# The low halves of the experts' weights formed on GpSimd instead of VectorE, except for the first expert's first matrix

## The chip, the cores and the metric

The kernel runs on one core of a Trainium2 chip. The metric is the device time of one execution in microseconds (us), the median of several runs. The names of the engines are those of the profile: PE is TensorE (PEld its weight loads), DVE is VectorE, ACT is ScalarE, POOL is GpSimd, SP is SyncE. L820 is line 820 of the kernel.

## The reference

The input of 8 sequences of 2496 tokens with 256 channels is filtered in the frequency domain, and the 19968 tokens that result are each sent to one of 8 experts, at most 2496 to each, in the order of their logits. An expert is two matrix products with a ReLU between them.

```python
X = np.fft.rfft(x, axis=1)
y = np.fft.irfft(X * (filt_r + 1j * filt_i)[None], n=2496, axis=1)
x = y.reshape(19968, 256)
logits = x @ w_gate                       # 8 experts
# greedy assignment: largest logits first, at most 2496 tokens for each expert
for e in range(8):
    mask = assigned == e
    out[mask] = np.maximum(x[mask] @ w1[e], 0.0) @ w2[e]
```

## The kernel before

The first part, up to about 400 us, transforms, filters and transforms back, and computes the logits. The second part is the experts, one after the other, and this is where the change lies. In it PE's instructions stand in the order in which the code issues them; the orders on DVE, ACT and POOL come from a scheduler that goes by its own estimates of time.

All products are made in a format with fewer mantissa bits, and to keep the accuracy each operand is split in two: a high half (the operand rounded to the format) and a low half (the operand minus its high half). A product is then three matmuls: high by high, high by low, low by high.

The weights of expert `e` are fetched with two indirect DMAs issued on POOL (L810, tiles `wr`): 128 partitions by 2048 elements for each of the two matrices. `Ffn.split` then makes the halves in eight parts of 512 columns, four for the first matrix and four for the second. For a part ACT writes the high half (L819, tiles `w0h` and `w1h`), and the low half is the difference (L820, `w0l` and `w1l`). The halves have two buffers each, so those of the next expert are made while PE still works on this one. The list `split` is worked off one part at a time between PE's steps, the first matrix's four parts first.

An expert's 2496 tokens are taken in five groups, four of 512 and one of 448. POOL gathers a group's rows with four indirect DMAs (L826, `xg`), PE transposes them (L840, `ptr`), and ACT and DVE split the result (L843 `xo`, L844 `z`). `first` makes eight products with the first matrix (L862, `pz`); for each, ACT writes the high half of the ReLU (L868) and DVE the low half (L870, or L873 in two pieces for the last group; tile `hl`). Then come the products with the second matrix (L905, `py`), the copy to `y` on ACT (L915) and the scatter to the output with an indirect DMA on POOL (L916).

While expert `e` runs, the assignment for the next one is made on DVE, with small matmuls on PE in between (`Route.phase` and `places`): rounds of counting with `Gm` (L553) and `rt` (L561, L574), then a table of tokens in five chunks (L757 to L789) that ends in the indices `xid`, for which the gathers wait. Some long DVE instructions over the logits belong to it: L638, L640, L642, L645 and L649. All of this falls mostly at the change from one expert to the next, when the new weights are split too.

So POOL's queue in the second part holds the weight loads (L810), the gathers (L826) and the scatters (L916), and DVE's queue holds the low halves of weights, of inputs and of ReLUs together with the assignment. Each engine works its own queue strictly in order.

Of the kernel before, what the change touches and what calls it, by code (L numbers as in the profile page):

```python
# [7 lines left out]
F32, F32R = mybir.dt.float32, mybir.dt.float32r  # L8
BF, F16, I32 = mybir.dt.bfloat16, mybir.dt.float16, mybir.dt.int32
AF, OP, AX = mybir.ActivationFunctionType, mybir.AluOpType, mybir.AxisListType  # L10
# [123 lines left out]
class Fft:  # L134
# [132 lines left out]
    def split(s, b, q, v, eng):  # L267
        y = s.yd[b, q] = [s.wp.tile([128, 2, D], F32R, name=n, bufs=3) for n in ("yh", "yl")]
        s.nc.scalar.copy(y[0], v)
        eng.tensor_tensor(y[1], v, y[0].bitcast(F32), op=OP.subtract)  # L270
# [522 lines left out]
class Ffn:  # L793
# [18 lines left out]
    def split(s, e, part):  # L812

        nc = s.nc
        raw, hl = s.wt[e]
        k, h = divmod(part, 4)
        o = 512 * (h if k else 2 * (h % 2) + h // 2)
        src, hi, lo = (t[:, o:o+512] for t in (raw[k], *hl[k]))
        nc.scalar.copy(hi, src)  # L819
        nc.vector.tensor_tensor(lo, src, hi.bitcast(F32), op=OP.subtract)  # L820

    def gather(s, e, g, ids):
        for t in range(4*g, 4*g + 4):
# [103 lines left out]
def emit(tc, i, out):  # L927
    nc = tc.nc
    with ExitStack() as st:
# [91 lines left out]
        while len(split) > 6:  # L1021
            W.split(*split.pop(0))
# [8 lines left out]
        with tc.manual_schedule(engines={mybir.EngineType.PE}):  # L1031
            pump.until((0, 1))
            p = ps.tile([128, 2, 256], F32, name="ptr", tag="c", bufs=4)
            for _ in range(12):
                nc.tensor.matmul(p[:, 0, :128], hot, hot, start=True, stop=True)
            for h in range(2):
                R.last = W.turn(0, 0, h)
            with tc.issue_after(R.last):
                while len(split) > 2:
                    W.split(*split.pop(0))  # L1040
            for e in range(8):
                pump.limit = e + 1
                def hook(what):
                    if what == 'w2':
                        flush(8)
                    elif isinstance(what, tuple):
                        gather(e, what[1])
                    elif e < 7:
                        if what == 'last':
                            gather(e + 1, 0)  # L1050
                            flush(4)
                        else:
                            W.turn(e + 1, 0, what - 1)
                for pe in W.run(e, pump, hook):
                    pump.feed(pe)
                    n += 1

                    if split and n % PACE == 0:
                        with tc.issue_after(W.lasta):
                            W.split(*split.pop(0))  # L1060
# [85 lines left out]
```

## Time and profile before

| what | value |
|---|---|
| median of 3 runs | 1422.28 us (1421.41 to 1422.91) |
| the profiled execution | 1421.22 us, of which the span is 1419.4 us |
| TensorE clock granted, mean of the span | 0.991 of full speed |
| PE busy | 1381.1 us, 97% of the span |
| DVE busy | 892.7 us, 63% |
| ACT busy | 675.1 us, 48% |
| POOL busy | 482.4 us, 34% |

The table is to be read with care: busy shares are averages over the span, and the parts of it differ. PE is near full throughout; what can still change the end is the little time in which it waits.

### The profile page before, as it was taken

The numbers are of one execution on the slowest core, as the hardware profiler recorded it, in microseconds if no ns is written. First come the engines' busy times: TensorE is split into PE (matmuls) and PEld (weight loads), VectorE is DVE, ScalarE is ACT, GpSimd is POOL, SyncE is SP. The second block draws the span as 40 slices with busy tenths as digits, with TensorE's granted clock in tenths as the row PEclk, the third lists the DMA queues.
The fourth block names the chain that finished last, engine by engine and source line by source line (L and its number), as shares of the span: only waits on it lengthen the run. The fifth ranks groups of instructions, "written<-read, shape, count | busy, mean of one in ns | idle before, by whom it ended". The sixth has DMA issues, their size and how long they took to land.

```text
span 1419.4 us, 27197 instructions
## 1 busy us (share of the span) xinstructions
PE 1381.1 (97%) x10362; PEld 1212.0 (85%) x10362; DVE 892.7 (63%) x2548; ACT 675.1 (48%) x1638; POOL 482.4 (34%) x539
## 2 busy tenths in 40 slices
PE   9999999999969999999999999999999999999998
PEld 8998898975438897898888989898898999899988
DVE  5577676775556768758757876876867635423231
ACT  6766666645455236326425534633723635423231
POOL 3343343431024125323531632433333323323312
PEclk9999999999989999999999999999999999999999
DMA  9665664537882022102212212112111321111100
GB/s 376 242 232 180 203 212 136 162 141 248 300 297 70 21 82 69 41 27 94 62 40 75 73 44 82 53 47 91 54 38 49 127 67 52 47 42 51 39 20 29
DMA packets 56532, 153.11 MB, mean 108 GB/s; under 512 B 9409, under 2 KB 29905, under 8 KB 52817
## 3 DMA queue, kind: packets, MB, share of 16 engines
q1 hardware_dynamic: 28072, 69.46, 14.0%
q0 software_dynamic: 18416, 60.37, 12.9%
q10 hardware_dynamic: 9913, 21.53, 4.3%
q8 instruction: 82, 1.34, 0.4%
q14 instruction: 49, 0.40, 0.1%
HBM read 88.32 MB, written 63.06 MB: 107 GB/s over the span
## 4 chain that ended last, share of the span: by engine, by line
PE 84%; issue 6%; DVE 4%; DMA 3%; ACT 2%; POOL 1%; POOLq 0%; ACTq 0%; DVEq 0%
PE py L905 27%; PE pz L862 27%; PE p L213 5%; PE p L229 5%; PE pv L393 4%; PE pa L284 4%; PE pa L248 2%; PE rt L561 2%; PE ptr L840 2%; PE pv L257 2%; POOL out L916 1%; DMA z<-zd 1%; PE rt L772 1%; DVE hl L873 1%; DMA wr<-w,widx 1%
## 5 line engine op out<-in xcount | busy, mean ns | idle before, releaser
L905 PE MATMUL py<-w1h,hl 128*128 128x256 f32 x2496 | 483.7, 286 | 1.1 <-DVE hl L873 1.0
L905 PEld LDWEIGHTS py<-w1h,hl 128*128 128x128 f32 x2496 | 401.3, 191 | 4.3 <-DVE hl L873 1.9
L905 PE MATMUL py<-w1l,hl 128*128 128x256 f32 (+1 forms) x1280 | 358.9, 282 | 0.0
L916 POOL DMA_INDIRECT out<-y,oid x160 | 167.0, 1044 | 490.1 <-ACT y L915 431.1
L868 ACT ACTIVATE hl<-pz 128x512 fp32r<-128x512 f32 (+1 forms) x320 | 188.1, 588 | 233.1 <-PE pz L862 208.2
L862 PE MATMUL pz<-xo,w0h 128*128 128x512 f32 (+1 forms) x640 | 263.3, 411 | 3.3 <-DVE dr L736 1.6
L870 DVE SCALAR_TENSOR_TENSOR hl<-pz,hl 128x512 fp32r<-128x512 f32 x256 | 175.1, 687 | 130.5 <-ACT hl L868 129.2
L862 PE MATMUL pz<-z,w0h 128*128 128x512 f32 (+1 forms) x640 | 248.6, 388 | 0.6 <-DVE z L844 0.6
L862 PE MATMUL pz<-xo,w0l 128*128 128x512 f32 (+1 forms) x640 | 248.4, 388 | 0.0
L905 PEld LDWEIGHTS py<-w1l,hl 128*128 128x128 f32 (+1 forms) x1280 | 240.9, 188 | 2.0
L826 POOL DMA_INDIRECT xg<-xs,xid x160 | 166.6, 1041 | 134.1 <-issue 55.7
L915 ACT COPY y<-py 128x256 f32<-128x256 f32 x152 | 56.6, 372 | 298.6 <-PE py L905 252.4
L862 PEld LDWEIGHTS pz<-xo,w0l 128*128 128x128 f32 x640 | 120.6, 188 | 23.8
L862 PEld LDWEIGHTS pz<-xo,w0h 128*128 128x128 f32 x640 | 121.5, 190 | 20.9 <-issue 2.1
L862 PEld LDWEIGHTS pz<-z,w0h 128*128 128x128 f32 x640 | 121.5, 190 | 16.8 <-DVE z L844 1.6
L219 ACT COPY Y<-p 64x240 f32<-64x240 f32 (+1 forms) x302 | 115.3, 382 | 29.3 <-PE p L213 22.2
L237 POOL TENSOR_TENSOR P<-P 128x256 f32<-128x256 f32 x80 | 58.7, 734 | 163.1 <-DVE P L235 162.9
L553 DVE TENSOR_TENSOR Gm<-M,thr 117x1232 bf16<-117x1232 f32 (+2 forms) x80 | 105.5, 1329 | 0.2
L213 PE MATMUL p<-cS,xr 117*128 117x120 f32 x688 | 93.9, 276 | 2.7 <-ACT Y L219 1.5
L213 PEld LDWEIGHTS p<-cS,xr 117*128 117x128 f32 x688 | 85.4, 191 | 6.8 <-ACT Y L219 4.3
L229 PE MATMUL p<-cW,Y 128*128 128x128 f32 x640 | 88.4, 276 | 0.6 <-DVE Q L236 0.6
L229 PEld LDWEIGHTS p<-cW,Y 128*128 128x128 f32 x640 | 80.0, 191 | 5.7 <-issue 3.9
(221 smaller groups left out, 1992.5 us busy)
## 6 DMA issues: line engine op xcount, KB each, us to landing
z<-zd SPq DMA_DIRECT2D x26, 600.0 KB
zd<-zt SPq DMA_DIRECT2D x60, 256.0 KB
xs<-xo ACTq DMA_DIRECT2D x18, 600.0 KB
xr<-x SPq DMA_DIRECT2D x6, 1536.0 KB
xr<-x SPq DMA_DIRECT2D x6, 1216.0 KB
zd<-zt ACTq DMA_DIRECT2D x20, 256.0 KB
xs<-xo SPq DMA_DIRECT2D x8, 600.0 KB
xr<-x SPq DMA_DIRECT2D x8, 512.0 KB
```

What stands on the lines that cost most here:

```text
L213: s.lastmm = nc.tensor.matmul(p[:, q-q0, :120], xv[:, q-24*h], s.cS1, start=True, stop=True).ins
L219: c = (nc.vector.tensor_copy if (t == 5 if b else cp) else nc.scalar.copy)(dst, src)
L229: nc.tensor.matmul(p[:, k], s.Y1[b][:, 4*g+k, dh*128:dh*128+128], s.cW[:, 4*g+k], start=True, stop=True)
L237: nc.gpsimd.tensor_tensor(P[:, :, :64], P[:, :, :64], P[:, :, 64:], op=OP.subtract)
L284: s.nc.tensor.matmul(p, w, v, start=m == 0, stop=m == 2)
L553: nc.vector.tensor_tensor(Gm[:, s0:s1, :m], s.M[:, s0:s1].unsqueeze(2).to_broadcast([117, s1 - s0, m]), thr[:117].unsqueeze(1).to_broadcas ...
L826: s.lastg = s.nc.gpsimd.indirect_dma_start(out=xg[:n], out_offset=None, in_=s.xs, in_offset=bass.IndirectOffsetOnAxis(ap=ids[0][:n, t:t+1] ...
L862: nc.tensor.matmul(p[:, :n], w[:, sl], x[:, k, :n], start=m == 0, stop=m == 5)
L868: s.lasta = s.R.relu = nc.scalar.activation(h[:, :n], p[:, :n], AF.Relu).ins
L870: s.R.low = nc.vector.scalar_tensor_tensor(l[:, :n], p[:, :n], 0.0, h[:, :n].bitcast(F32), op0=OP.max, op1=OP.subtract).ins
L905: nc.tensor.matmul(p[:a.stop-a.start], hs[g][f][:, a], b[:, 256*f:256*f+256], start=m == 0, stop=m == 8 * len(terms) - 1, skip_group_check ...
L916: st = nc.gpsimd.indirect_dma_start(out=out_rows, out_offset=bass.IndirectOffsetOnAxis(ap=ids[1][:w, 4*g+t:4*g+t+1], axis=0), in_=y[:w], i ...
```

## The change

The low half of a weight part is formed on POOL instead of DVE, for the second matrix of every expert and for the first matrix of all experts but the first. That is 60 instructions of 64; four, of the first expert's first matrix, stay on DVE. The operation, its operands and the high halves on ACT are as before.

```diff
         src, hi, lo = (t[:, o:o+512] for t in (raw[k], *hl[k]))
         nc.scalar.copy(hi, src)
-        nc.vector.tensor_tensor(lo, src, hi.bitcast(F32), op=OP.subtract)
+        (nc.gpsimd if e or k else nc.vector).tensor_tensor(lo, src, hi.bitcast(F32), op=OP.subtract)
```

The scheduler sets the orders anew. PE's and SP's are the same as before; those of POOL, DVE and, a little, ACT are not. On POOL, from the weight loads for the second expert on (`wr_6577` and `wr_6578` are its two raw matrices), the rows before were:

```order
L810 DMA wr_6577<-w,widx 128x2048
L810 DMA wr_6578<-w,widx 128x2048
L916 DMA out<-y,oid 19968x256 x4
L826 DMA xg<-xs,xid 128x256 x4
L916 DMA out<-y,oid 19968x256
L826 DMA xg<-xs,xid 128x256 x4
L916 DMA out<-y,oid 19968x256 x2
```

After the change the same place reads as follows, from behind the two weight loads on.

```order
L916 DMA out<-y,oid 19968x256 x2
L820 TENSOR_TENSOR w0l<-wr_6577,w0h 128x512 x2
L916 DMA out<-y,oid 19968x256
L820 TENSOR_TENSOR w0l<-wr_6577,w0h 128x512
L916 DMA out<-y,oid 19968x256
L826 DMA xg<-xs,xid 128x256 x4
L820 TENSOR_TENSOR w0l<-wr_6577,w0h 128x512
L820 TENSOR_TENSOR w1l<-wr_6578,w1h 128x512 x2
L916 DMA out<-y,oid 19968x256
L820 TENSOR_TENSOR w1l<-wr_6578,w1h 128x512
L916 DMA out<-y,oid 19968x256
L826 DMA xg<-xs,xid 128x256 x4
```

Eight low halves have come into POOL's queue, three ahead of the first gathers of the new expert and four more ahead of the second; the eighth stands behind those. On DVE, at the same change of experts and behind the low halves of the last group's ReLUs (`hl`), the rows before were:

```order
L737 TENSOR_TENSOR r<-r_6451,dr 128x8
L820 TENSOR_TENSOR w1l<-wr_6578,w1h 128x512
L773 TENSOR_TENSOR loc<-sidx,rt 128x2
L873 SCALAR_TENSOR_TENSOR hl<-pz,hl 128x64
L873 SCALAR_TENSOR_TENSOR hl<-pz,hl 128x384
L873 SCALAR_TENSOR_TENSOR hl<-pz,hl 128x64
L873 SCALAR_TENSOR_TENSOR hl<-pz,hl 128x384
L773 TENSOR_TENSOR loc<-sidx,rt 128x2
L765 TENSOR_SCALAR GE<-iota,BC 117x512
L873 SCALAR_TENSOR_TENSOR hl<-pz,hl 128x64
L873 SCALAR_TENSOR_TENSOR hl<-pz,hl 128x384
L727 TENSOR_TENSOR asg<-asg,u_6713 117x176
```

And with the change, from the same L737 on:

```order
L737 TENSOR_TENSOR r<-r_6451,dr 128x8
L773 TENSOR_TENSOR loc<-sidx,rt 128x2
L873 SCALAR_TENSOR_TENSOR hl<-pz,hl 128x64
L873 SCALAR_TENSOR_TENSOR hl<-pz,hl 128x384
L873 SCALAR_TENSOR_TENSOR hl<-pz,hl 128x64
L873 SCALAR_TENSOR_TENSOR hl<-pz,hl 128x384
L773 TENSOR_TENSOR loc<-sidx,rt 128x2
L765 TENSOR_SCALAR GE<-iota,BC 117x512
L727 TENSOR_TENSOR asg<-asg,u_6713 117x176
L733 TENSOR_TENSOR val<-val,a_6718 128x8
L873 SCALAR_TENSOR_TENSOR hl<-pz,hl 128x64
L873 SCALAR_TENSOR_TENSOR hl<-pz,hl 128x384
```

The low half of the weights is gone from between L737 and L773, and the last pair of ReLU halves now stands behind L727 and L733.

## Rows read from the trace of the kernel before

**Rows 1.** The page: busy time and share of the span, by engine.

```profile
PE 1381.1 (97%) x10362; PEld 1212.0 (85%) x10362; DVE 892.7 (63%) x2548; ACT 675.1 (48%) x1638; POOL 482.4 (34%) x539
```

**Rows 2.** Windows: stretch, its length, busy time of each engine, clock, DMA.

```profile
539.20:557.20 18.00, 15.66 (x115) 14.20 (x115) 17.75 (x59) 9.47 (x31) 10.34 (x9) 1.00 0.22 67
...
1200.00:1300.00 100.00, 100.00 (x679) 92.23 (x678) 31.78 (x89) 35.69 (x88) 32.33 (x34) 1.00 0.13 42
```

**Rows 3.** PE's timeline behind 440 us: every wait, in brackets with its releaser.

```profile
540.05 0.44 PE L862 MATMUL pz<-xo,w0h 128*128 128x448 f32 x1 [1.59 <-DVE dr L736]
...
545.71 0.50 PE L905 MATMUL py<-w1h,hl 128*128 128x256 f32 x2 [0.70 <-DVE hl L873]
...
547.24 0.50 PE L905 MATMUL py<-w1h,hl 128*128 128x256 f32 x2 [0.30 <-DVE hl L873]
...
557.31 0.50 PE L862 MATMUL pz<-z,w0h 128*128 128x512 f32 x1 [0.59 <-DVE z L844]
...
569.67 0.64 PE L561 MATMUL rt<-A,Gm 117*128 117x96 bf16 x11 [0.89 <-DVE Gm L553]
...
671.87 0.33 PE L772 MATMUL rt<-dt,GE 117*128 117x180 f16 x2 [1.49 <-DVE ex L777]
...
896.78 0.51 PE L862 MATMUL pz<-xo,w0h 128*128 128x512 f32 x1 [0.98 <-DVE loc L773]
...
919.75 0.42 PE L561 MATMUL rt<-A,Gm 117*128 117x48 bf16 x10 [0.38 <-DVE ex L777]
...
1025.87 0.45 PE L561 MATMUL rt<-A,Gm 117*48 117x32 bf16 x11 [0.94 <-DVE ex L777]
```

**Rows 4.** Line 820: count, ns (min/median/max), starts; DVE's idle time before it.

```profile
L820 DVE TENSOR_TENSOR w0l<-wr,w0h x32: 675/684/721, 419.3 to 1196.4; 128x512 fp32r<-128x512 f32 x32
...
  ACT w0h L819: 15.9, 11
```

**Rows 5.** Groups on POOL by form: count, busy us, mean ns, idle before.

```profile
L270 POOL TENSOR_TENSOR yl<-Y,yh 128x512 fp32r<-128x512 f32 x4 | 5.0, 1277 | 16.9 <-PE pa L284 14.9 <-ACT yh L269 2.0
```

**Rows 6.** DVE's timeline: start and length in us.

```profile
329.84 1.02 DVE L589 TENSOR_TENSOR thr<-km,ic 128x7 int32<-128x7 int32 x1
330.90 2.58 DVE L553 TENSOR_TENSOR Gm<-M,thr 117x560 bf16<-117x560 f32 x2
...
454.51 0.17 DVE L589 TENSOR_TENSOR thr<-km,ic 128x7 int32<-128x7 int32 x1
...
544.32 0.67 DVE L820 TENSOR_TENSOR w1l<-wr,w1h 128x512 fp32r<-128x512 f32 x1
544.92 0.14 DVE L773 TENSOR_TENSOR loc<-sidx,rt 128x2 f32<-128x2 f32 x1
```

**Rows 7.** POOL's timeline at the same place as the first two rows of group 6.

```profile
329.55 1.29 POOL L270 TENSOR_TENSOR yl<-Y,yh 128x512 fp32r<-128x512 f32 x1 [1.95 <-ACT yh L269]
331.50 1.26 POOL L270 TENSOR_TENSOR yl<-P,yh 128x512 fp32r<-128x512 f32 x1 [0.66 <-PE pa L284]
```

**Rows 8.** Groups on DVE from 539.2 to 557.2 us: busy us, mean ns.

```profile
L873 DVE SCALAR_TENSOR_TENSOR hl<-pz,hl 128x64 fp32r<-128x64 f32 (+1 forms) x12 | 4.0, 372 | 0.0
L820 DVE TENSOR_TENSOR w1l<-wr,w1h 128x512 fp32r<-128x512 f32 x4 | 2.7, 674 | 0.0
L640 DVE TENSOR_TENSOR tmp<-lg,M 117x1408 f32<-117x1408 f32 x1 | 1.6, 1606 | 0.0
```

**Rows 9.** POOL's timeline: gathers for the second expert.

```profile
541.71 2.45 POOL L826 DMA_INDIRECT xg<-xs,xid  x1 [0.30 <-PE pz L862]
...
550.99 0.97 POOL L826 DMA_INDIRECT xg<-xs,xid  x1 [1.68 <-PE ptr L840]
```

**Rows 10.** Timelines of ACT and PE at three places.

```profile
433.16 0.61 ACT L819 CAST w1h<-wr 128x512 fp32r<-128x512 f32 x1
...
440.30 0.28 PE L905 MATMUL py<-w1l,hl 128*128 128x256 f32 x1
...
562.54 0.60 PE L840 MATMUL ptr<-id,xg 128*128 128x128 f32 x4
```

## The prediction, made before the changed kernel ran

> **What bounds the kernel now.** I read the page first for the busy shares [rows 1]: PE is busy 97% of the span, no other engine more than 63%. So PE's own work sets the time, and since the change leaves PE's instructions and their order as they are, it can reach the end only through the time in which PE waits. The reader should therefore look next not at DVE's 893 us but at PE's timeline in the part that the change touches, from about 440 us on, and pick out the rows with a bracket [rows 3]. There are nine. They add up to 1.59 + 0.70 + 0.30 + 0.59 + 0.89 + 1.49 + 0.98 + 0.38 + 0.94 = 7.86 us, and in every one the releaser is DVE. They come in bunches: five between 540 and 570 (first to second expert), one at 672, two around 900 to 920, one at 1026, each at a change of experts. The windows view says why [rows 2]: from 539.2 to 557.2 DVE is busy 17.75 us of 18, while between 1200 and 1300, when no weights are split for a next expert and the counting is over, it is busy 31.8 of 100 and PE waits for nothing. So DVE is the limit for some 18 us at a time, at the changes of experts, and nowhere else behind 440 us. Of those 18 us five low halves of weights are a part: the four of the second matrix, 2.7 us of busy time [rows 8], and the last one of the first matrix.
>
> All that is to be gained is hence at most 7.9 us of 1422, 0.55%. A measurement of this kernel tells about 0.2%, 2.84 us, from no change.
>
> **What is removed.** Sixty low halves leave DVE. The instruction is 0.68 us long in the median [rows 4], but the next one starts a little before it ends: 0.60 us after it at 544.32 [rows 6]. So one takes 0.60 us of DVE's queue, and 60 of them are 36 us, nearly all of it work beside which PE runs on. DVE also sat idle for 15.9 us in front of eleven of the `w0l` [rows 4], which tells that the first ones of an expert come at a time when DVE has nothing else to do: taking those away gives PE nothing. What counts is the last five of an expert, which stand in the full stretch: 5 x 0.60 = 3.0 us. The first expert's four that move (the second matrix) have no wait of PE near them: no row of [rows 3] lies before 540.
>
> **What is added on POOL.** The same operation in the same shape, 128x512 with two float operands in SBUF, stands in the trace on POOL already, in L270: 1.277 us [rows 5]. Sixty are 77 us, on an engine busy 34% of the span [rows 1]. That is cover enough on average; the question is what stands behind them in the queue. These are scatters, for which nobody waits soon, and gathers. The second four gathers of the second expert begin at 550.99 us [rows 9], and PE transposes the first of them at 562.54 [rows 10]: from the end of the first issue 10.6 us, for a transfer and for whatever comes in between. The order puts four low halves between the first and the second four gathers, 4 x 1.28 = 5.1 us. They fit, even if POOL were idle for none of it; cost nothing, with some 5 us to spare. For the first expert, ACT's last cast of the second matrix starts at 433.16 and takes 0.61; one POOL instruction later it is 435.1, and PE first reads a low half of that matrix at 440.30 [rows 10]: nothing. The low halves of the later experts are made before the expert begins or during its first group, ahead of their use; nothing again. If the cover went, a gather that is late by 1 us would cost PE 1 us, at each of up to seven changes.
>
> **What is added on DVE.** Here is the cost that the diff does not show. At 329.55 POOL starts its subtraction of 1.29 us, so it ends at 330.84 [rows 7]. At 329.84 DVE starts L589, a 7-column instruction with both operands in SBUF that takes 0.17 us elsewhere, and this time takes 1.02 us: it ends at 330.86 [rows 6]. Then come two L553 of 560 columns, again with two operands in SBUF; together they take 2.58 us, and POOL's next subtraction runs from 331.50 to 332.76 in the middle of them, at its usual 1.26 us. By size their 1120 columns should take 1.28 us (L640 with 1408 takes 1.606 [rows 8]); 1.30 us are too much, which is POOL's whole instruction. So while POOL subtracts, a DVE instruction with two SBUF operands stands still till POOL is done, and DVE's strict order holds everything behind it.
>
> The Trainium skill says the same in "SBUF — State Buffer", section "Who interferes with whom": a DVE instruction with two SBUF inputs contends with a GpSimd instruction that reads SBUF, since its second input comes through the interface they share, and the one that comes second is held off in full. It speaks against this change; by it a move of work between these two engines pays in one and is charged in the other. On one point the trace shows more than that page: it has descriptor generation untouched by such DVE instructions, while the gather at 541.71 took 2.45 us beside L640 [rows 9].
>
> How much of the 1.28 us is charged? In the full stretch DVE's 15 us besides the weights are about half instructions with two SBUF operands (L640 with 1.6 us, L642 with as many columns, L649, L553, and some fifteen small ones; about 7 us by my addition) and half others (the ReLU halves L873, which read PSUM and one SBUF tile, 4.0 us [rows 8], the reduction L645 over as many columns as L640, L844; about 8 us). The first kind comes some twenty times in 15 us. Nothing is charged if DVE happens to have free work for 1.28 us, all of it if the next instruction is of the first kind. Free work comes in some nine runs of 8/9 = 0.9 us, but behind about half of the twenty there is no run at all, so at a random place about 0.45 us of free work come before the next one that is blocked: the charge is 1.28 - 0.45 = 0.83, I take 0.8 us. Its bounds are 0 and 1.28.
>
> **The sum.** In a full stretch five low halves save 0.6 us and cost 0.8 us each: DVE is late by 1 us more at its end. PE pays this where it already waits for DVE, at four changes (540 to 570, 672, 900 to 920, 1026) [rows 3]; at the others it has some slack. 4 x 5 x (0.8 - 0.6) = +4.0 us. Against the profiled execution that is 1421.22 + 4.0 = 1425.2 us; the median of the runs shown is 1.06 us above that execution, so the forecast is 1426.3, in round numbers 1426 us, slower by 0.3%. By the bounds of the charge the sum would be 20 x (0 - 0.6), capped by the waits that can go, to 20 x (1.28 - 0.6) = +13.6 us.
>
> **The rivals.**
> - *The charge and the saving cancel.* If POOL's subtractions mostly begin beside a ReLU half or L645, the charge is near 0.6 us, and the time is 1422 to 1423, with the waits only shuffled. For it: the two numbers are close, and half of DVE's work is free. Against it: nothing in particular. Within 0.2% as long as the charge lies between 0.46 and 0.74 (0.6 -+ 2.84 / 20).
> - *Faster: the relief wins.* Place: the waits at 545.71, 547.24, 557.31, 671.87, 896.78, 919.75 and 1025.87. In front of L873, L844, L777 and L773, which release them, DVE's queue holds a low half; together they are 5.38 us. (The first, 1.59 us, is behind L638, which stays, and the 0.89 us before `Gm` comes after all low halves.) If POOL starts its subtractions where DVE reads PSUM, these go: 1422.28 - 5.4 = 1416.9 us; with half of them 1419.6. The price decides: below 0.46 us of charge per instruction it is faster by more than can be doubted. Against it: twenty two-operand instructions in 15 us leave POOL few gaps of 1.28 us.
> - *Much slower: subtractions in a row.* The order has three low halves in a row behind the first four gathers. If POOL goes from one to the next without letting DVE in, a two-operand instruction that comes right behind the start stands for 3 x 1.28 = 3.8 us, and the `hl` behind it, for which PE waits at 545.71. Saved up to there are two low halves, 1.2 us, so PE loses 2.6 us at such a change; at five of them 13 us, 1435 us. That the second L553 had to let POOL in, and not the reverse, says that whoever is there first goes first; a row of them is not in the trace.
> - *Gathers late*, as priced above: needs more than 5 us of delay on POOL; unlikely. That the change does not do what it says can be ruled out by the order: 60 instructions have moved.
>
> **How the numbers follow.** Charge above saving, slower by more than 0.2%: 0.43, of which the row of subtractions and late gathers have about 0.1; its likeliest time is 1426. Cancel, within 0.2%: 0.35. Relief, faster by more than 0.2%: 0.22. The range runs from half of the relief, 1418.5, to the slower case with most of a row of subtractions, 1433; outside I leave about 0.1 on each side. The slower case alone has 1425 to 1435.
>
> **What would show it.** Right: L820 on POOL at about 1.28 us, not longer; on DVE the small two-operand instructions at the changes of experts (L727, L733, L737, L785) with single lengths of up to 1.3 us, as L589 had in [rows 6]; PE's waits between 540 and 1030 above 7.9 us in sum, still with DVE as releaser. Wrong: those DVE lengths unchanged, and the waits of the second rival gone; or a wait of PE for `xg`, or for a low half by POOL, which I hold for hidden. What would make it wrong: that POOL's subtractions fall into gaps of the two-operand work, or that the new order on DVE, which puts some ReLU halves behind L727 and L733 and some assignment ahead, matters more than the port.

## The result, and the profile after

The changed kernel takes 1439.42 us (median, 1439.03 to 1440.52) where the kernel before takes 1421.88 us (1421.41 to 1422.91): ratio 1.0129, 95% interval 1.0116 to 1.0142. It is slower by 17.5 us; the forecast was slower by 4, with a range that ended at 1433.

The page of the changed kernel, the line that answers to [rows 1]:

```profile
PE 1390.7 (97%) x10362; PEld 1219.2 (85%) x10362; DVE 896.8 (62%) x2488; ACT 674.1 (47%) x1638; POOL 559.3 (39%) x599
```

The groups of line 820 on POOL, in the columns of [rows 4]:

```profile
L820 POOL TENSOR_TENSOR w1l<-wr,w1h x32: 1255/1294/1323, 430.2 to 1219.1; 128x512 fp32r<-128x512 f32 x32
L820 POOL TENSOR_TENSOR w0l<-wr,w0h x28: 1279/1300/1325, 531.8 to 1214.0; 128x512 fp32r<-128x512 f32 x28
```

Two things are to be seen. The subtraction on POOL takes 1.29 to 1.30 us, as forecast from [rows 5]. And DVE's busy time has not fallen, though 60 instructions have left it: 896.8 us against 892.7. Its other instructions have become longer.

PE's waits behind 440 us are now 21, with 17.35 us in sum, where [rows 3] has nine with 7.86. Those of over 1 us, from PE's timeline (in brackets the wait and its releaser):

```profile
549.15 0.79 PE L905 MATMUL py<-w1h,hl 128*128 128x256 f32 x2 [3.39 <-DVE hl L873]
...
676.56 0.33 PE L772 MATMUL rt<-dt,GE 117*128 117x180 f16 x2 [1.06 <-DVE ex L777]
...
684.84 0.79 PE L905 MATMUL py<-w1h,hl 128*128 128x256 f32 x2 [1.59 <-DVE loc L773]
...
808.42 0.44 PE L862 MATMUL pz<-xo,w0h 128*128 128x448 f32 x1 [1.01 <-DVE hl L873]
...
915.93 0.32 PE L772 MATMUL rt<-dt,GE 117*128 117x180 f16 x2 [1.41 <-DVE ex L777]
...
1036.13 0.71 PE L840 MATMUL ptr<-id,xg 128*128 128x128 f32 x4 [1.53 <-DVE hl L870]
...
1146.62 0.32 PE L772 MATMUL rt<-dt,GE 117*128 117x180 f16 x2 [1.45 <-DVE pf L705]
```

The releaser is DVE in every one; no wait is for a gather or for a low half of the weights. (The transposition at 1036.13 reads `xg`, but it waits for its buffer in PSUM, which `hl` frees: L870 ends at 1036.08.) The 3.39 us stand three matmuls ahead of the place where [rows 3] has 0.70 us at 545.71, in the same product; the matmul that now waits began at 544.50 in the kernel before, without a wait. What DVE and POOL did in front of it, from the timeline:

```profile
542.73 1.99 POOL L826 DMA_INDIRECT xg<-xs,xid  x1 [0.30 <-PE pz L862]
...
544.14 4.36 DVE L732 TENSOR_TENSOR a<-a,b 128x8 f32<-128x8 f32 x1
...
544.75 1.29 POOL L820 TENSOR_TENSOR w0l<-wr,w0h 128x512 fp32r<-128x512 f32 x1
...
545.99 2.47 POOL L820 TENSOR_TENSOR w1l<-wr,w1h 128x512 fp32r<-128x512 f32 x2
548.42 0.68 DVE L873 SCALAR_TENSOR_TENSOR hl<-pz,hl 128x64 fp32r<-128x64 f32 x2
```

L732, 8 columns wide, takes 0.15 us elsewhere. Here it arrives at 544.14, while POOL still issues a gather, and ends at 548.50, when the third of three subtractions has ended (548.46). Behind it in DVE's queue stands the `hl` for which PE waits. In the windows, the line that answers to the first of [rows 2], at the same place of the program, DVE is nearly as full as before (16.94 us against 17.75), and PE less:

```profile
541.90:559.90 18.00, 14.41 (x92) 13.43 (x91) 16.94 (x40) 7.61 (x25) 10.81 (x9) 0.81 0.12 37
```

A smaller case is more frequent: an instruction arrives during a DMA issue of POOL's, and stands until the one subtraction behind that issue has ended.

```profile
801.82 0.99 POOL L916 DMA_INDIRECT out<-y,oid  x1 [0.17 <-DVE ar L645]
802.28 1.89 DVE L782 SCALAR_TENSOR_TENSOR xid<-ex,js 128x4 int32<-128x4 f32 x1
802.83 1.31 POOL L820 TENSOR_TENSOR w1l<-wr,w1h 128x512 fp32r<-128x512 f32 x1
```

Behind 440 us, 26 DVE instructions are longer than the median of their kind by over 0.5 us (holds, from here on), by some 37 us in sum. In the kernel before there is none. Twelve of them, with 21.0 us, arrived during a DMA issue. Thirteen are of kinds with one tensor operand (`tensor_scalar` and casts: L765, L781, L729, L603, L623).

PE's clock falls behind the longest waits. Windows, PE only: stretch, its length, PE's busy time, granted clock, DMA:

```profile
545.00:550.00 5.00, 1.61 (x11) 0.82 0.09 26
550.00:555.00 5.00, 4.79 (x23) 0.50 0.04 15
555.00:560.00 5.00, 5.00 (x45) 0.99 0.12 41
680.00:685.00 5.00, 2.30 (x15) 0.98 0.08 25
685.00:690.00 5.00, 5.00 (x32) 0.68 0.26 80
```

After the 3.39 us of waiting PE runs at 0.50, which is 1.2 of its 2.4 GHz, for some 6 us, to 555.06. In [rows 2] the same stretch has 1.00 throughout, with the 1.59 us wait of [rows 3] in it.

Where the time goes is read best from the start of one kind of row that both kernels have in the same order: PE's transpositions (L840). The table gives how much later they start than in the profile of before that the prediction used, at a place inside each expert. "Before, again" is a second profile of the kernel before.

```
start in      before, changed change  lows    POOL    gathers halves
before        again   kernel  again   by ACT  memsets behind  (256)
513.98        +1.76   +2.74   +2.59   +1.69   +1.69   +1.68   +1.61
618.93        +0.20   +5.12   +4.92   +1.09   +3.38   -0.05   +2.57
745.98        +0.18   +9.79   +9.58   +0.10   +2.05   +4.87   +6.52
870.52        +0.19  +12.01  +11.81   +0.09   +3.65   +9.18   +8.80
995.47        +0.20  +14.31  +13.87   -0.52   +2.78  +10.88  +10.01
1095.81       +0.20  +15.30  +14.86   -0.84   +1.70  +14.75  +10.07
1238.86       +0.19  +18.24  +17.80   -0.51   +1.59  +16.06  +10.88
```

Between the changes of experts nothing is lost; at them it is: about 4, 4.7, 2.2, 2.3 and 1.0 us, and 2.9 us for the last two together (2.6 and 0.3). The 2.7 us of the first line are no loss: a second profile of before has 1.8 of them, and gives them back at the first change, where PE waited anyway.

### The profile page after: what moved, and what is told of

Same layout as the page of the kernel before. It is cut to its first block, busy times and chain, and to the rows that moved or that the text cites. A ratio compares the mean times of both kernels' runs of the same rounds, so it can differ in the third digit from the quotient of the medians.

```text
span 1437.2 us, 27209 instructions
## 1 busy us (share of the span) xinstructions
PE 1390.7 (97%) x10362; PEld 1219.2 (85%) x10362; DVE 896.8 (62%) x2488; ACT 674.1 (47%) x1638; POOL 559.3 (39%) x599
## 3 DMA queue, kind: packets, MB, share of 16 engines
q0 software_dynamic: 18416, 60.37, 12.8%
## 4 chain that ended last, share of the span: by engine, by line
PE 78%; DVE 8%; issue 6%; ACT 3%; DMA 3%; POOL 1%; POOLq 0%; ACTq 0%; DVEq 0%
PE py L905 25%; PE pz L862 24%; PE p L213 5%; PE p L229 5%; PE pa L284 4%; PE pv L393 3%; PE pa L248 2%; PE rt L561 2%; PE ptr L840 2%; DMA z<-zd 2%; PE pv L257 2%; POOL out L916 1%; ACT junka L776 1%; DVE hl L873 1%; DVE hl L870 1%
## 5 line engine op out<-in xcount | busy, mean ns | idle before, releaser
L870 DVE SCALAR_TENSOR_TENSOR hl<-pz,hl 128x512 fp32r<-128x512 f32 x256 | 175.0, 688 | 137.4 <-ACT hl L868 136.1
L776 ACT ACTIVATE junka<-rt,loc 128x176 bf16<-128x176 f32 x160 | 65.7, 411 | 44.0 <-DVE loc L773 37.7
```

The source lines that it names most:

```text
L776: nc.scalar.activation(s.junka, pr[:, h, :S], AF.Sign, bias=loc[:, c:c+1], scale=-1.0, accum_out=js[:, c:c+1])
L870: s.R.low = nc.vector.scalar_tensor_tensor(l[:, :n], p[:, :n], 0.0, h[:, :n].bitcast(F32), op0=OP.max, op1=OP.subtract).ins
```

## Experiments

Two theories at the outset. *Port*: POOL's reading of SBUF stops DVE, with its variant *rows* (DVE is not let in between two subtractions of a row, that is, of several that follow each other on POOL). *Order*: the scheduler's new order on DVE, or what stands behind the subtractions on POOL, costs the time. After the first trials a third was formed, *queue*: subtractions that stand ready behind a DMA issue on POOL stop DVE from that issue to the end of their row. Four runs (second trials, filled wait, each matrix alone) were made on another chip, on which the kernel before takes 1450.57 us; of them ratios are used, and stretches at full clock.

**All on DVE, and on POOL as well.**

```
 nc.vector.tensor_tensor(lo, src, hi, op=OP.subtract)
+if e or k:
+    nc.gpsimd.tensor_tensor(scr, src, hi, op=OP.subtract)
```

> The kernel before, with all 64 low halves on DVE, and POOL makes the 60 subtractions as well, into a scratch tile that nobody reads. Theory port (POOL's subtractions stop DVE): nothing is saved and everything is charged, so at least the loss of the change, 17.5 us: 1439 to 1460 us, with small DVE instructions of 2 to 4 us. Rival order (the scheduler's other order on DVE costs the time, or the gathers behind the subtractions): the order on DVE is nearly that of before, so 1422 to 1425 us.

1464.12 us, ratio 1.0303 (1.0283 to 1.0323). DVE is busy 948.2 us, 55.5 more than in [rows 1], with as many instructions. Sixty subtractions that nobody reads cost 42 us, a little more than the range had. DVE's order is that of before but for two rows, and of PE's 24 waits behind 440 us, 35.45 us in sum, 23 are for DVE and one for ACT, none for a gather. Theory port holds.

**Memsets in place of the subtractions.**

```
-nc.gpsimd.tensor_tensor(lo, src, hi, op=OP.subtract)
+nc.gpsimd.memset(lo.bitcast(F32), 0.0)
+nc.gpsimd.memset(lo.bitcast(F32), 0.0)
```

> The changed kernel with the same order on DVE and ACT, but on POOL two memsets of 128x512 stand in place of each of the 60 subtractions: POOL reads nothing, the low halves are zeros. Theory port (it is the reading of SBUF by POOL that stops DVE): the 60 instructions are gone from DVE and nothing is charged, so 1415 to 1423 us, and no DVE instruction is stretched near L820. Rival order: as the changed kernel, 1436 to 1440 us. If memsets hold DVE as well, between the two, by their length.

1420.99 us, ratio 0.9994 (0.9984 to 1.0004). DVE's order is that of the changed kernel to the row, and its loss is gone: theory order falls. Memsets hold some of DVE's instructions too, the 16-bit `tensor_scalar` L765 for 2.48 us instead of 0.34:

```profile
543.64 1.94 POOL L1151 MEMSET w0l<- 128x512 f32 x4
...
545.12 2.48 DVE L765 TENSOR_SCALAR GE<-iota,BC 117x512 f16<-117x512 f16 x1
...
545.50 1.95 POOL L1152 MEMSET w0l<- 128x512 f32 x4
```

The trace has eight such holds of over 0.5 us, with 13.4 us in sum, and the time of the whole is that of before all the same.

**A gap behind each subtraction.**

```
 nc.gpsimd.tensor_tensor(lo, src, hi, op=OP.subtract)
+nc.gpsimd.memset(gap, 0.0)          # 128x128
```

> The changed kernel, with a memset of a 128x128 scratch tile (0.20 us in the trace of before) behind each of POOL's 60 subtractions, so that no two subtractions stand back to back. Theory rows (DVE isn't let in between two subtractions that follow each other at once, but is in any gap): single DVE instructions of at most 1.5 us, the 4.36 us of L732 gone; rows of two to four stand at four changes and cost about 2.6 us each, so 1427 to 1433 us. Rival single charges (each subtraction stops DVE for its own length whatever the spacing): 1438 to 1442 us.

1437.57 us, ratio 1.0109 (1.0093 to 1.0126). A gap of 0.2 us frees almost nothing; L732 takes 4.38 us again. That the rows need only be broken up is refuted in this form.

**First trials behind the kernel's end.**

```
V.memset(src[:, :8], 1.0)               # lets POOL's row start
V.tensor_copy(big[:, :512], psum)       # 0.68 us
for _ in range(2): V.tensor_tensor(t, S, T, op=OP.subtract)   # 8 columns, or another kind
for j in range(row): g.tensor_tensor(lo[:, 512*j:512*j+512], src, hi, op=OP.subtract)
```

> The kernel before with trials behind its end: DVE copies 512 columns from PSUM while POOL begins 1, 2, 3, 4 or 6 subtractions of 128x512, then DVE does two small instructions of one kind. Theory rows: the two-operand tensor_tensor of 8 columns waits to the end of the whole row: about 0.7, 1.9, 3.2, 4.5 and 7 us instead of 0.15; with a memset between the subtractions only to the end of the current one, below 1.3 us. By the trace of the changed kernel a one-operand tensor_scalar that writes 16-bit values is held too; instructions that read PSUM or only reduce are not (0.15 and 0.7 us). Rival: each subtraction lets DVE in, and every trial with x2 shows at most 1.3 us.

With rows of 2, 3, 4 and 6 alike, the first small instruction stands to the end of the current subtraction, the second to the end of the next. Timelines of POOL and DVE for the row of three, and under them, from the view of that line, the single lengths of the two (ns min/median/max):

```profile
1424.46 3.70 POOL L1200 TENSOR_TENSOR w0h<-wr,wr 128x512 f32<-128x512 f32 x3 [0.21 <-DVE wr L1194]
...
1424.89 2.07 DVE L1173 TENSOR_TENSOR w1l<-w1h 128x8 f32<-128x8 f32 x2
```

```profile
L1173 DVE TENSOR_TENSOR w1l<-w1h x2: 852/1019/1186, 1424.9 to 1425.8; 128x8 f32<-128x8 f32 x2
```

So here DVE is let in at each end of a subtraction, for one instruction, and my theory rows was wrong for this case. Held in the same way (2.07 to 2.52 us for the two) were `tensor_scalar`, copy and cast from SBUF to SBUF; not held were a reduction (0.35), a memset (0.20), and whatever reads PSUM (0.36). With a memset of 128 columns (0.20 us) between the subtractions the second was let in as well (0.17 us), with one of 8 or 32 columns not. Why then 4.36 us in the kernel?

**Second trials: a gather ahead of the row.**

```
+g.indirect_dma_start(out=slot, ...)    # ahead of the row on POOL
```

> The kernel before with a second set of trials behind its end: POOL issues a gather (0.97 us) and then 0, 1 or 3 subtractions, DVE does 512-column copies from PSUM and then two small instructions, which arrive during the gather or during the first subtraction. Theory queue (a subtraction that stands ready behind a POOL instruction already counts, so DVE is stopped from the gather on and through the whole row): the first small instruction behind gather and three subtractions takes about 0.2 + 3 x 1.25 = 4 us, behind gather and one 1.5 us, behind a gather alone 0.15. Rival boundary (DVE is let in at each end of a subtraction, as in the first trials): 1.5 us with one and with three. The 4.36 us of L732 in the changed kernel speak for the first, the trials without a gather for the second.

Behind a gather and three subtractions the two small instructions take 4.47 us, two `tensor_scalar` as long; without the gather the two take 2.03. Of the 4.47 us the second has 4.28: the first began 0.24 us after the start of the gather's issue and took 0.16, the second came 0.43 us after that start and stood to the end of the row. So the hold does not begin with the issue but inside it. Arriving when the gather is over, in the first subtraction, it still takes 3.02 us, to the end of the row. With 128-column memsets between the subtractions the second takes 4.58. Behind a gather and one subtraction, the first takes 1.94. Theory queue holds.

**Third trials.**

> The kernel before with a third set of trials behind its end, all with a gather on POOL and DVE's two small two-operand instructions arriving during it. Theory queue (what stands ready behind the gather takes the port from DVE until POOL's queue is empty or waits): gather and one subtraction about 2 us for the pair, gather and three 4.5 us, gather and twelve subtractions of 64 columns up to the end of the twelfth, gather alone 0.36; with the second and third subtraction waiting for DVE itself the first small instruction about 2 us at most. Three one-operand copies on POOL hold them too, three memsets don't hold two-operand instructions but hold a tensor_scalar. Rival: only subtractions of full width, or only the first one, hold DVE: 2 us in each of these trials.

A gather alone and, once more, a gather and three subtractions, from the timelines, and under them the single lengths of the latter's two:

```profile
1477.37 0.96 POOL L1209 DMA_INDIRECT w0l<-xs,xid  x1 [4.66 <-DVE w0l L1201]
1477.71 0.36 DVE L1174 TENSOR_TENSOR w1l<-w1h 128x8 f32<-128x8 f32 x2
...
1482.60 0.95 POOL L1209 DMA_INDIRECT w0l<-xs,xid  x1 [4.27 <-DVE w0l L1201]
1482.94 4.56 DVE L1174 TENSOR_TENSOR w1l<-w1h 128x8 f32<-128x8 f32 x2
...
1483.57 3.70 POOL L1211 TENSOR_TENSOR w0h<-wr,wr 128x512 f32<-128x512 f32 x3
```

```profile
L1174 DVE TENSOR_TENSOR w1l<-w1h x2: 166/2264/4361, 1482.9 to 1487.3; 128x8 f32<-128x8 f32 x2
```

The first takes 4.361 us: the 4.36 us of L732, made at will. It came 0.34 us after the start of the gather's issue. A gather alone holds nothing. Where the subtraction behind the gather waited for DVE itself, the two small instructions took 0.15 and 0.17 us: only what stands ready holds. Three memsets behind a gather hold a `tensor_scalar` for 2.11 us and two-operand instructions not at all. Against the theory: twelve subtractions of 64 columns held DVE to the end of the gather only (0.63 us for the two), and three one-operand copies of POOL's let DVE in between (0.63 us for the first instruction, to the end of the gather, and 1.16 for the second).

**The gathers behind the row.**

```
 if what == 'last':
-    gather(e + 1, 0)
     flush(4)
+    with tc.issue_after(W.lastp): gather(e + 1, 0)   # lastp: the last low half
```

> The changed kernel with the first four gathers of the next expert put behind the low halves of that place on POOL, so that the row of three at the first change stands no longer behind a gather as a whole; two rows of other changes get longer. The order on DVE stays. Theory queue: L732's 4.36 us at the first change falls below 2.7 us and PE's wait of 3.39 us with it, without the clock at half: 2 to 4 us less at the first change, the whole 1434 to 1440 us, since the other changes keep their rows behind scatters. Rival boundary: no difference, 1438 to 1441 us. If gathers are late, PE waits for xg and it is slower than the changed kernel.

1436.16 us, ratio 1.0097 (1.0082 to 1.0112), beside 1438.31 of the changed kernel on the same chip (1.0116, 1.0101 to 1.013: the intervals overlap, so it is the trace that tells). The order on DVE is the same but for two rows. At the first change the wait of 3.39 us is 0.64, and PE's offset goes from +1.68 to -0.05 there, where the changed kernel's goes from +2.59 to +4.92; at later changes, where subtractions now fall together otherwise, part of it is lost again (PE waits 2.10 us at 671, 2.81 at 800 and 2.69 at 907).

**The wait filled.**

```
+for _ in range(26): nc.tensor.matmul(p, zero, b[:, :256], start=False, stop=False)
 nc.tensor.matmul(p, hs[g][f][:, a], ...)    # the matmul that waits 3.39 us
```

> The changed kernel with 26 matmuls of 256 columns by a tile of zeros (26 x 0.12 = 3.1 us) on PE in the place of its longest wait (3.39 us at 549.15), so that PE works while it waits; the sum stays the same. Theory clock (the wait brings PE's granted clock to half for about 5 us, on top of its own length): the clock stays at 1.00 between 545 and 560 and the change from first to second expert costs about 2 us less than the 2.4 to 3.2 us of the changed kernel; the whole 1437 us. Rival: the clock has nothing to do with it and PE stands at the same offset behind the change.

Ratio 1.0079 (1.0062 to 1.0096). The windows of PE, as above:

```profile
545.00:550.00 5.00, 5.00 (x36) 1.00 0.29 82
550.00:555.00 5.00, 4.24 (x31) 1.00 0.01 2
555.00:560.00 5.00, 5.00 (x43) 1.00 0.07 26
```

The clock stays at full, though the hold is there: 4.31 us, here at L726; ten rows of DVE's order differ. From the last matmul ahead of the wait to the next transposition PE takes 9.25 us (549.02 to 558.27), the fillers included, and in the changed kernel 11.00 (545.49 to 556.49): 1.75 us of the loss there were the clock. The changed kernel itself was not run on that chip, so the whole's ratio isn't to be compared with 1.0129 to such a size.

**Each matrix alone**, `e and not k` and `e and k` for `e or k`:

> Only the low halves of the first matrix of experts 1 to 7 on POOL, 28 instructions, the others on DVE. Theory port: three of each four are made while DVE has slack, one stands in the full stretch, alone or ahead of nothing, so 7 charges of up to 2 us against a saving of 0.6 each: 1423 to 1429 us. Rival: the loss goes with the number of instructions, 28/60 of 17.5 us: 1430 us. For the pair of this and the next run, theory port with rows says that together they lose less than the change does, since rows of three come only when both are on POOL.

> Only the low halves of the second matrix of experts 1 to 7 on POOL, 28 instructions. Theory port: all four stand in or near the full stretch, two of them in a row behind gathers: 7 x (1 to 1.7) us, 1428 to 1434 us, clearly more than with the first matrix. Rival: by number, 1430 us, the same as with the first matrix.

Ratios 1.0048 (1.0032 to 1.0065) and 1.0065 (1.0048 to 1.0082). The difference between them is inside their intervals, so these two don't tell the place from the number; their sum, 0.0113, is not clearly below the 0.0129 that the whole change has on other chips. What theory port with rows expected of the pair is not shown.

**The first expert's alone**, `k and not e`:

> Only the first expert's second matrix (four low halves) on POOL. By the prediction's step (no wait of PE near them) and by theory queue (DVE has slack there) it costs nothing: 1420 to 1423 us. Rival: the 2.6 us by which PE stood later behind 434 us belong to these four: 1424 to 1425 us.

> The kernel before once more, for a second profile. In all kernels of this study on the first chip PE stands 1.7 to 3 us later at 430 us than in the one profile of before (once 5 to 6), ahead of the first moved instruction. If that is chance of the transfers ahead of 420 us, this second profile stands later by up to 3 us too; if it is the change, it stands at 419.1 and 430.4 us as the first.

1421.63 us, ratio 0.9999 (0.9989 to 1.0009): these four cost nothing. The second profile of before starts its transpositions 1.8 to 2.1 us later at 419 to 434 us, so the early offset is chance.

**What the removal is worth: the low halves by ACT.**

```
-nc.vector.tensor_tensor(lo, src, hi, op=OP.subtract)
+nc.scalar.copy(lo, src)
```

> The kernel before, with the 60 low halves replaced by second copies of the raw weights on ACT (0.6 us each, so they hold the raw weights and not the rest): DVE loses its 60 instructions and POOL gets none. It prices what the change could have gained at most. Theory relief (DVE's low halves in front of what PE waits for cost up to 5.4 us): 1416 to 1420 us. Rival no relief (the waits come from the other work of DVE): 1421 to 1424 us, or more if ACT's copies delay the ReLUs.

1419.80 us, ratio 0.9985 (0.9976 to 0.9994): 1.6 us faster (0.9 to 3.4 by the interval), at the upper end of what theory relief expected. PE's waits are 5.65 us in sum, one of them (0.44 us) for ACT, against 7.86 in the first profile of before and 6.27 in the second. The page's line, with DVE without the 60 and without anything held by them:

```profile
PE 1382.9 (97%) x10362; PEld 1213.7 (86%) x10362; DVE 859.1 (61%) x2488; ACT 702.9 (50%) x1698; POOL 479.2 (34%) x539
```

**The change again.**

> The changed kernel once more, beside the three others on the same chip: 1.0129 times the kernel before by all theories. Its profile tells which of the waits of the first profile come again: by theory queue the hold of 4.36 us at the first change, since it depends on the order only; the 2.75 us by which PE stood later between 434 and 514 us, which arose before the first moved instruction ran, should be chance and come out different.

1438.31 us, ratio 1.0116 (1.0101 to 1.013). L732 takes 4.37 us, PE's waits are 17.24 us in sum: the holds come again with the order, so they are not chance.

**Shorter pieces**, the subtraction cut into pieces of 64, 128 and 256 columns:

```
+for c in range(0, 512, 64):
+    nc.gpsimd.tensor_tensor(lo[:, c:c+64], src[:, c:c+64], hi[:, c:c+64], op=OP.subtract)
```

> The changed kernel with each of POOL's 60 subtractions cut into eight of 64 columns (12 of these took 3.35 us in the third trials, so one low half takes about 2.2 us of POOL instead of 1.28). Theory length of the single POOL instruction (twelve short ones behind a gather held DVE for 0.3 us only, three long ones for 4.36): no DVE instruction is held by more than about 0.5 us, PE's wait of 3.39 us is gone, and what is left is the relief, at most 1.6 us: 1419 to 1425 us. Rival total time on the port (what counts is how long POOL subtracts behind a gather): 77 us have become 134, so slower than the changed kernel, 1440 to 1455 us. If gathers come late behind rows of 6 us, PE waits for xg: 1425 to 1432 us.

> The same in four pieces of 128 columns. Theory length: between the change and the run with 64 columns, 1421 to 1432 us. Rival total time on the port: 1440 us or more. If a row is held as a whole whatever the pieces, long DVE instructions of over 4 us show beside the rows of pieces.

> The same in two pieces of 256 columns. Theory length: nearer to the change, 1428 to 1440 us; rival: 1438 us or more. With the change itself (512 columns, 1438.3 us on another occasion) the three runs give the loss against the length of a POOL instruction: falling by theory, flat or rising by the rival.

1475.89, 1442.38 and 1431.51 us; ratios 1.0387 (1.0364 to 1.041), 1.0152 (1.0135 to 1.0169), 1.0068 (1.005 to 1.0086). With 64 columns a 4-column instruction stands for 12.8 us before 48 pieces behind a gather:

```profile
1238.05 0.95 POOL L826 DMA_INDIRECT xg<-xs,xid  x1 [0.30 <-issue]
1239.03 4.50 POOL L1152 TENSOR_TENSOR w0l<-wr,w0h 128x64 fp32r<-128x64 f32 x16
1239.06 12.80 DVE L782 SCALAR_TENSOR_TENSOR xid<-ex,js 128x4 int32<-128x4 f32 x1
...
1243.50 8.92 POOL L1152 TENSOR_TENSOR w1l<-wr,w1h 128x64 fp32r<-128x64 f32 x32
```

So the length of the single instruction is not what holds, against my theory; here it is the time of the ready row. (In the trial with twelve such pieces DVE's instruction arrived inside the gather's issue, here 0.03 us behind the first piece's start; whether that is the difference is not shown.) Halves are the exception: in the row at the first change L765 stands for 0.95 us only, and L727 and L733 behind it for 0.86 and 0.68, each let in after one piece or so; PE waits 2.30 us there. Neither theory gives a minimum at 256 columns. When DVE is let in within a row stays open.

No version that computes the low halves was faster than the kernel before. The run by ACT, which pays 28 us of ACT's time for its copies, puts what is to be had at about 1.6 us, at most 3.4 by its interval.

## Why the prediction missed

The direction was right, and so was the kind of mechanism (DVE held by POOL's subtractions); the size was not, and neither was the form of the holds. The forecast of +4 us was a charge of 16 less a saving of 12; measured were +17.5 with a saving of 1.6. By its own steps:

- **What bounds it: right.** The loss lies at changes of experts, PE waits for DVE alone. But not at four changes: six of seven lost 1 us or more. Those near 800 and 1130, where [rows 3] has no wait, had less slack than the holds needed.
- **POOL's price and cover: right.** 1.29 to 1.30 us, no wait for a gather or a low half, the first expert's free (0.9999).
- **What is removed: the saving was over-valued.** This is the step that failed most: "five low halves save 0.6 us and cost 0.8 us each", 4 x 5 x (0.8 - 0.6). DVE did lose 892.7 - 859.1 = 33.6 us of work, 0.56 us each. But the sum let 20 x 0.6 = 12 us of it reach PE, when the waits that could go at all were 5.4 us by the prediction's own second rival. The run by ACT puts it at 1.6 us, and the memset run, with holds of its own, gains less still (0.9994). The low halves stood mostly where PE did not wait for what came behind them.
- **What is added on DVE: near in sum, wrong in form.** The charge on DVE is DVE's busy time of the changed kernel less that of the run by ACT: 896.8 - 859.1 = 37.7 us, 0.63 us for each of 60. What PE pays for it is known by difference only, 17.5 + 1.6 = 19 us; the prediction's 20 x 0.8 was 16. That the two lie near is luck: the 16 are twenty charges of at most 1.28 us at four changes, the 19 come from 26 holds of up to 4.2 us at more changes than four, and a part of them is the clock. And the bound of 1.28 us per subtraction was too low: the hold can begin in the DMA issue ahead (1.89 us at 802.28 for one subtraction) and run through a row (4.36 us).
- **Which instructions are held: half of them were missed.** The prediction counted those with two SBUF operands. The trials and 13 of the 26 holds show `tensor_scalar` and casts with one. The Trainium skill names copy, cast and `tensor_scalar` as operations that can contend, beside the two-input form, in "SBUF — State Buffer", section "Who interferes with whom"; the trace agrees (2.07 us for two copies of 8 columns beside a row, 0.35 for two reductions), and I took only the half of that passage that [rows 6] showed.
- **The rival "subtractions in a row": nearest to what came, at 0.1 (with late gathers) far too low.** It named the place and the 3.8 us, and L732 stood 4.36. Its ground was not enough: in the trials a row alone let DVE in at each end, and a row behind a DMA issue did not. That "a row of them is not in the trace" was true; but POOL's order did show three low halves in a row behind four gathers. The rival gave 1435 us with the saving still credited.
- **A term that was absent: the clock.** 1.75 us at the first change, and by estimate about as much at the second: the window 685 to 690 at 0.68 lacks 0.32 x 5 = 1.6 us. PE's waits are longer by 9.5 us than in the first profile of before, and by 11.1 than in the second, whose eight waits sum to 6.27. With the second that makes some 14.5 of the 17.5. Most of the rest lies at the waits as well: by the starts of the same matmuls in both traces PE falls back there by about 0.16 us more than the bracket says (1.17 at the wait of 1.01 us, 1.69 at that of 1.53), and there are 13 more of them, 2 us. Gaps too short for the list are not it: those under 0.15 us fall from 0.26 us in sum to 0.16. About 1 us stays open.
- **Rivals cancel and relief: refuted** by the whole loss. The 5.4 us of relief are more than the bare removal gives (0.9985, at most 3.4 us).

## What to carry to other kernels

Before work is moved off an engine that is busy but not the bound, price the removal by itself: cap it by the waits whose releaser stands directly behind the removed instructions, and set it against the charge only up to that cap. Before elementwise work goes to POOL, look at what stands ahead of it there: in this kernel and in the trials ready subtractions behind a DMA issue stopped DVE's SBUF-to-SBUF instructions from inside the issue to the end of the row, and a cut into pieces changed the loss either way (10 us with 256 columns, 54 with 64). A busy sum that does not fall when instructions leave is the first sign of holds; the median of each group against its longest finds them.

## What the runs showed of the hardware

- One small DVE instruction stood 4.36 us behind a gather and three POOL subtractions, 0.85 us beside the same row without a gather (let in at the first end), and was not held by a gather alone (0.36 us for two). Behind a gather and three subtractions an instruction that began 0.24 us after the start of the gather's issue was free (0.16 us), one that came at 0.34 us was held.
- A hold needs ready work: with the subtraction waiting for DVE, 0.15 us.
- POOL's memsets hold `tensor_scalar` (2.11 us) but no two-operand subtraction (0.35 us for two). The Trainium skill, in "SBUF — State Buffer", section "Who interferes with whom", has a two-input instruction contend with POOL's reads and not with what only writes; the trials agree.
- Pieces of 64 columns: DVE held to the end of the gather only in the trial, 12.8 us in the kernel; of 256: for about one piece (0.68 to 0.95 us). Not explained.
- A wait of 3.39 us was followed by some 6 us at clock 0.50. One of 1.59 us at 540.05 in the kernel before was not; one of 1.59 us at 684.84 in the changed kernel, behind waits of 0.82 and 0.29 us, was followed by a window at 0.68.
